# The order of VectorE's work at the second layer's first seven-product pair: one weight sum and two weight splits moved ahead of and between four output blocks

## The chip, the cores and the metric

The kernel runs on one core of one Trainium2 chip. The metric is the device time of one execution in microseconds (us); the figure for the kernel before is the median of three executions. Beside these times stands one profiled execution, of which every instruction's start and length is recorded.

## The reference, cut to what matters

The computation is one block of a network with two stages, each with a layer norm ahead of it and a modulation drawn from a small vector `c`. The first stage is a gated long convolution over the 2048 tokens. The second, in which the change lies, mixes tokens:

```python
def _B_ref(x, w1, b1, w2, b2):
    h = _layernorm(x, axis=-1)                 # (1, 2048 tokens, 640 channels)
    u = jnp.einsum("bsd,sf->bdf", h, w1) + b1  # first layer, F = 1728
    u = _gelu(u)
    y = jnp.einsum("bdf,fs->bds", u, w2) + b2  # second layer, back to 2048 tokens
    return transpose(y, 0, 2, 1)
...
h = _layernorm(x, axis=-1) * (1 + cb) + sb
x = x + gb * _B_ref(h, B_w1, B_b1, B_w2, B_b2)
```

All inputs and outputs are float32. In the kernel's second layer the output for 128 tokens and 640 channels is a product of a slice of `w2` (the stationary operand) with `u` (the moving operand), summed over 14 blocks of 128 values of F; then `b2` is added, the sum is multiplied by `gb`, and `x` is added.

## The kernel before

**Precision.** TensorE multiplies in a reduced float32 format. Each operand is therefore kept as two parts: a high part, written by ScalarE as a copy into that format, and a rest, written by VectorE as the operand less the high part. A product of two operands is three matmuls: high with high, high with rest, rest with high (`product`, L1046). Making the two parts of a weight tile is a `split` (L1034 on ScalarE, then a subtraction on VectorE). All of VectorE's two-operand work goes through one helper, so it carries line L57 whatever it computes.

**The second layer in two parts.** The 16 blocks of 128 output tokens are done in two ways. The first four (`for s in range(NW)`, matmuls on L1123) are plain products, each into a PSUM bank pair of its own, `acc[0]` to `acc[3]`. The other twelve are done two at a time, in six pairs, and each pair by seven products in place of eight (a Strassen-like scheme): the weights of a pair are cut into four blocks, A11, A12, A21 and A22, sums of them (S1 to S4) are made on VectorE, and seven products named in `ORDER` are run, 42 in all. They are numbered here as in the code, from 0: product 0 is A11, 1 is A12, 2 is S1, 3 is S2, 4 is S3, 5 is S4, 6 is A22, and product 7 begins the next pair. The change's "sixth sum" is that of product 5, its "fifth and sixth splits" those of products 4 and 5. One product is 7 blocks of F times 3 matmuls, 21 matmuls of 128x320.

**What one product needs.** `sums(n)` makes the weight sum of product n where it has one: one subtraction or addition for S1 and S4, two for S2 (which make S3's too), none for the others. `split(n)` fills one of three weight slots, slot n modulo 3, so it can start once product n - 3 is done. `product(n)` runs the matmuls into a PSUM bank. There are four banks in turn (the ring of L811); products 0 and 1 share one, 2 and 3 another. The two that hold `acc[2]` and `acc[3]` come next in turn, so product 4 writes where `acc[2]` lay and product 5 where `acc[3]` lay.

**Outputs.** `outcome(n)` combines product n's result with those before. Four of the seven products of a pair end in `finish`: add the bias, (add a partial result,) multiply by `gb`, add `x`, and issue the store on SyncE's queue. This is three VectorE instructions where a partial result is added and two where not. `acc[2]` and `acc[3]` are still to be finished when the 42 products start: that is four calls of `finish`, two instructions each, on the tiles `o2, o4, o3, o1` in turn. These are "VectorE's four blocks". The first instruction of each (L1053) is the one that reads PSUM.

**Order.** Nothing reorders the instructions: the schedule is manual, and each engine works through its instructions in the order in which the program was written, waiting on semaphores. In the loop over n, the sum of product n + 3 and the split of product n + 2 are written ahead of product n, and outcome(n) behind it. In the first pair, outcomes 0 and 2 are written behind products 1 and 3. The four finishes of `acc[2]` and `acc[3]` are written at n = 1, behind outcome 1. GpSimd makes the last set of moving sums (`t_ops(6, pool)`) as the loop begins.

Of the kernel before, what the change touches and what calls it, by code (L numbers as in the profile page):

```python
# [47 lines left out]
def mixer_kernel(ctx: ExitStack, tc: tile.TileContext, q, k, v, shift_k, ssm_k, ssm_D, w1, b1, w2, b2, c,  # L48
# [11 lines left out]
    def mem(tag, n, name=None):  # L60

        return sb.tile([128, n], F32, name=name or tag, tag=tag, bufs=1)
# [4 lines left out]
    def psum(slot=None):  # L67

        uid[0] += 1
        slot = ring[uid[0] % len(ring)] if slot is None else slot  # L70
        return psp.tile([128, 1024], F32, name=f"pst_{uid[0]}", tag=f"pst{slot}", bufs=1)
# [324 lines left out]
    def load_w(n, t=X):  # L396
        if n >= len(order):
            return
        i = order[n]
        if i < NF:  # L400
            t = j16(t)
            for b in range(2):
                sync.dma_start(t[64 * b:64 * b + 64],
                               dram(w1, 16 * b * F + fo(i), [[32 * F, 64], [F, 16], [1, 128]]))
            raw[i] = (t, [slice(0, 8), slice(8, 16)])
        else:
            t = f14(t)
            load_w2(t, i - NF, 0, 14)
            raw[i] = (t, [slice(0, 7), slice(7, 14)])
# [14 lines left out]
    def split_w(n, t2=None, eng=dve):  # L424
        if n >= len(order):
            return
        i = order[n]
        if t2 is None:
            t2 = T_wb[n % 2]
        view = j16 if i < NF else f14  # L430
        hi, lo = view(t2[:, 0:2048]), view(t2[:, 2048:4096])
        t, parts = raw.pop(i)
        for f in parts:
            act.activation(hi[:, f].bitcast(F32R), t[:, f], AF.Copy)
        for f in parts:
            TT(eng, lo[:, f].bitcast(F32R), t[:, f], hi[:, f], ALU.subtract)
        blk[i] = hi, lo
# [486 lines left out]
    def t_ops(i, eng=dve):  # L924

        def full(t, n, h):
            u = U[i + 7 * n]
            TT(eng, t, u[h], u[2 + h], ALU.add)

        def half(n, t):  # L930
            act.activation(TU[i][n][0].bitcast(F32R), t, AF.Copy)

        def rest(n, t):
            TT(eng, TU[i][n][1].bitcast(F32R), t, TU[i][n][0], ALU.subtract)

        a, b, c_ = RB
        full(a, 0, 0)
        full(b, 0, 1)
        TT(eng, a, b, a, ALU.subtract)
        half(0, a)  # L940
        full(c_, 1, 1)
        TT(eng, b, c_, b, ALU.subtract)
        half(2, b)
        TT(eng, c_, c_, a, ALU.subtract)
        half(1, c_)
        rest(0, a)
        full(a, 1, 0)
        TT(eng, a, a, c_, ALU.subtract)
        half(3, a)
        rest(2, b)  # L950
        rest(1, c_)
        rest(3, a)
# [42 lines left out]
    def load_pair(p, n0=0, n1=4):  # L995

        if p < NP:
            for n in range(n0, n1):
                w_ = ("A11", "A21", "A22", "A12")[n]
                A[p, w_] = place[(4 * p + n) % 8]  # L1000
                load_w2(A[p, w_], NW + 2 * p + int(w_[1] == "2"), 7 * int(w_[2] == "2"), 7)
# [4 lines left out]
    def x_pair(p):  # L1006
        if p < NP:
            for n in range(4):
                x_load(NW + 2 * p + n // 2, n % 2, xq[4 * (p % 2) + n])

    def sums(n):

        p, w_ = n // 7, ORDER[n % 7]
        if p >= NP:
            return
        a = lambda k: A[p, k]
        if w_ == "S1":
            A[p, w_] = S1
            TT(dve, S1, a("A21"), a("A22"), ALU.add)
        elif w_ == "S2":  # L1020
            TT(dve, a("A21"), a("A11"), a("A21"), ALU.subtract)
            TT(dve, a("A11"), S1, a("A11"), ALU.subtract)
            A[p, "S3"], A[p, "S2"] = a("A21"), a("A11")
        elif w_ == "S4":
            TT(dve, a("A12"), a("A12"), a("S2"), ALU.subtract)
            A[p, "S4"] = a("A12")

    def split(n):

        p, w_ = n // 7, ORDER[n % 7]  # L1030
        if p >= NP:
            return
        W[n] = slots[n % 3]
        act.activation(W[n][0].bitcast(F32R), A[p, w_], AF.Copy)  # L1034
        TT(dve, W[n][1].bitcast(F32R), A[p, w_], W[n][0], ALU.subtract)

    def product(n):
        w_ = ORDER[n % 7]
        if n > 4 or n % 2 == 0:
            bank["t"] = psum()  # L1040
        bank[n] = bank["t"][:, 0:320] if n > 3 or n % 2 == 0 else bank["t"][:, 512:832]
        wh, wl = W.pop(n)
        for i in range(7):
            rh, rl = moving[w_](i)
            for k, (w, r) in enumerate(((wh, rh), (wh, rl), (wl, rh))):
                pe.matmul(bank[n], w[:, i].bitcast(F32R), r.bitcast(F32R), start=i == 0 and k == 0,  # L1046
                          stop=i == 6 and k == 2)

    def finish(s, h, t, o, x, u=None):

        g = GB[:, 320 * h:320 * h + 320]
        if u is None:
            dve.scalar_tensor_tensor(o, t, B2C[:, s:s + 1], g, op0=ALU.add, op1=ALU.mult)  # L1053
        else:
            dve.scalar_tensor_tensor(o, t, B2C[:, s:s + 1], u, op0=ALU.add, op1=ALU.add)
            TT(dve, o, o, g, ALU.mult)
        TT(dve, o, o, x, ALU.add)
        sync.dma_start(out[128 * s:128 * s + 128, 320 * h:320 * h + 320], o)

    def outcome(n):  # L1060

        p, w_ = n // 7, ORDER[n % 7]
        t, s, x = bank.pop(n), NW + 2 * p, xq[4 * (p % 2):4 * (p % 2) + 4]
        if w_ == "A11":
            act.activation(p1, t, AF.Copy)
        elif w_ == "S1":
            act.activation(p5, t, AF.Copy)
        elif w_ == "A12":
            finish(s, 0, t, o1, x[0], p1)
        elif w_ == "S2":  # L1070
            TT(dve, u2, t, p1, ALU.add)
        elif w_ == "S3":
            TT(dve, u3, t, u2, ALU.add)
            TT(dve, u2, u2, p5, ALU.add)
            finish(s + 1, 1, u3, o4, x[3], p5)
            if p == NP - 1:
                TT(dve, u3, u3, GB[:, 0:320], ALU.mult)
                TT(dve, u3, u3, x[2], ALU.add)
        elif w_ == "S4":
            finish(s, 1, t, o2, x[1], u2)  # L1080
        elif p == NP - 1:
            finish(s + 1, 0, t, o3, u3)
        else:
            finish(s + 1, 0, t, o3, x[2], u3)
# [8 lines left out]
    def early(s):  # L1093

        for h in range(2):
            o, x, b2_ = RB[h], xe[2 * s + h], B2C[:, s:s + 1]
            dve.scalar_tensor_tensor(o, acc[s][:, h, 0:320], b2_, GB[:, 320 * h:320 * h + 320], op0=ALU.add, op1=ALU.mult)
            TT(dve, x, o, x, ALU.add)
            sync.dma_start(out[128 * s:128 * s + 128, 320 * h:320 * h + 320], x)

    for s in range(NW):
        i = NF + s
        acc.append(psum().rearrange("p (h m) -> p h m", h=2))
        split_w(i)
        load_w(i + 1)
        if s < 3:
            t_ops(3 + s)
        if s > 1:
            early(s - 2)
        if s == 3:  # L1110
            load_pair(1, 0, 3)
            m_w.append(mem("w1", 4096, "m_w0"))
            slots += [(q7(m_w[0], 1792 * i), q7(m_w[0], 1792 * i + 896)) for i in range(2)]
            split(0)
            split(1)
            sums(2)
            sums(3)
        wh, wl = blk[i]
        for f_ in range(NF):
            u = U[f_]  # L1120
            for k, (w, r) in enumerate(((wh, 0), (wh, 2), (wl, 0))):
                for h in range(2):
                    pe.matmul(acc[s][:, h, 0:320], w[:, f_].bitcast(F32R), u[r + h].bitcast(F32R),  # L1123
                              start=f_ == 0 and k == 0, stop=f_ == NF - 1 and k == 2)
# [9 lines left out]
    t_ops(6, pool)  # L1134
    load_pair(1, 3, 4)
    for n in range(7 * NP):
        if n:
            sums(n + 3)
        split(n + 2)
        product(n)  # L1140
        if n == 1 or n == 3:
            outcome(n - 1)
        if n != 0 and n != 2:
            outcome(n)
        if n == 1:
            for k in range(4):
                finish(2 + k // 2, k % 2, acc[2 + k // 2][:, k % 2, 0:320], (o2, o4, o3, o1)[k], xq[4 + k])
        if n == 2:
            x_pair(1)
        if n % 7 == 6:  # L1150
            load_pair(n // 7 + 2)
            x_pair(n // 7 + 2)
# [34 lines left out]
```

## Time and profile before

| | us |
|---|---|
| median of three executions | 681.57 |
| lowest and highest of them | 678.05 and 681.95 |
| the profiled execution | 683.93 |
| span of the profiled execution, first to last instruction | 682.1 |
| TensorE busy with matmuls (PE) | 629.4 |
| VectorE busy (DVE) | 498.3 |
| ScalarE busy (ACT) | 300.2 |
| GpSimd busy (POOL) | 133.9 |

PE is TensorE's matmuls, PEld its weight loads, DVE is VectorE, ACT ScalarE, POOL GpSimd, SPq SyncE's DMA queue. A row of the timeline has the start in us from the span's start, the length, engine, line, operation, tiles out<-in, shape and count (rows of one kind that follow each other are merged, so the start of the next row of that engine tells how long they held it), and in brackets how long the engine had been idle and what it waited for. A row of the table by windows has the stretch, its length, the busy time and instruction count of each engine, then the clock granted to TensorE as a share of full speed, the share of DMA time and GB/s. In this kernel `m_w` are the weight slots, `pst` PSUM banks, `m_x` the output, partial-result and x tiles, and `m_v`, `x` and `m_p` hold raw weight blocks and their sums.

### The profile page before, as it was taken

The page shows a single profiled execution, that of the slowest core. Times are in us where ns is not written, and L with a number is a line of the kernel's source. Part 1 is how long each engine was busy: PE and PEld are TensorE (multiplying, and loading weights), DVE is VectorE, ACT ScalarE, POOL GpSimd, SP SyncE. Part 2 cuts the span into 40 slices and gives each one's busy share as a digit, 9 for nine tenths or more (in the row PEclk, how much of TensorE's full clock was granted, in tenths as well). Part 3 has the DMA queues.
Part 4 walks back from the last instruction along what each step waited for, and adds up shares of the span by engine and source line. Part 5 has one row for each costly group of instructions (what it writes and reads, how often), then busy time and mean ns, then how long its engine had stood idle before and what let it go on. Part 6 is the DMA issues. An engine that isn't in the chain of part 4 may idle for free.

```text
span 682.1 us, 20757 instructions
## 1 busy us (share of the span) xinstructions
PE 629.4 (92%) x9119; PEld 598.4 (88%) x9119; DVE 498.3 (73%) x869; ACT 300.2 (44%) x483; POOL 133.9 (20%) x157
## 2 busy tenths in 40 slices
PE   6878778999999898798899999999999989999997
PEld 2877568899989897688899889999999989999997
DVE  7789589989898279798866622321689779888995
ACT  1654655646657265457654222322344133333331
POOL 6762067226134142000000000000000520000000
PEclk9998989999999799888899999999999999999999
DMA  9999797375426153440308333335441634355601
GB/s 188 219 260 274 246 179 157 91 138 121 66 65 215 35 134 104 91 97 1 62 1 154 62 63 63 62 64 115 120 136 55 197 114 124 102 167 166 184 32 38
DMA packets 166538, 81.23 MB, mean 119 GB/s; under 512 B 90830, under 2 KB 156912, under 8 KB 166448
## 3 DMA queue, kind: packets, MB, share of 16 engines
q1 hardware_dynamic: 159276, 78.32, 47.5%
q10 hardware_dynamic: 6916, 1.31, 1.1%
q8 instruction: 71, 1.16, 0.7%
q0 software_dynamic: 256, 0.28, 0.2%
q14 instruction: 19, 0.16, 0.1%
HBM read 69.40 MB, written 10.49 MB: 117 GB/s over the span
## 4 chain that ended last, share of the span: by engine, by line
PE 68%; DVE 14%; ACT 6%; DMA 5%; issue 3%; SPq 2%; POOL 1%; ACTq 0%; POOLq 0%; DVEq 0%
PE pst L445 20%; PE pst L1046 17%; PE pst L1123 7%; PE pst L223 7%; PE pst L242 6%; PE pst L271 5%; PE pst L291 3%; DVE p L57 3%; ACT z L280 2%; DMA in<-in_w_mod_dram 1%; PE pst L919 1%; DVE tap L57 1%; DMA y<-in_A_ssm_k_dram 1%; DVE sm L548 1%; DVE kt L57 1%
## 5 line engine op out<-in xcount | busy, mean ns | idle before, releaser
L242 PE MATMUL pst<-z,w 128*64 128x64 f32 x2560 | 78.4, 223 | 13.1 <-DVE p L57 6.7
L242 PEld LDWEIGHTS pst<-z,w 128*64 128x64 f32 x2560 | 76.4, 138 | 15.6 <-issue 9.1
L229 ACT ACTIVATE z<-pst 128x1024 f32<-128x1024 f32 (+2 forms) x45 | 43.1, 977 | 46.3 <-PE pst L223 46.2
L57 POOL TENSOR_TENSOR y<-p 128x256 f32<-128x256 f32 x72 | 51.3, 741 | 42.4 <-DVE p L57 42.1
L57 DVE TENSOR_TENSOR p<-pst,kt 128x512 f32<-128x512 f32 x80 | 50.7, 680 | 7.9 <-ACT kt L246 7.9
L1046 PE MATMUL pst<-r_z,m_w 128*128 128x320 f32 x222 | 42.0, 312 | 2.2 <-DVE m_w L57 2.2
L882 ACT ACTIVATE pst<-pst,sm 128x640 f32<-128x640 f32 x13 | 10.0, 767 | 75.9 <-PE pst L445 75.9
L271 PEld LDWEIGHTS pst<-v,y 32*128 32x128 f32 x1280 | 38.2, 187 | 5.4 <-issue 4.8
L271 PE MATMUL pst<-v,y 32*128 32x64 f32 x1280 | 40.1, 272 | 2.5 <-issue 2.3
L246 ACT ACTIVATE kt<-pst 128x512 f32<-128x512 f32 x40 | 24.0, 599 | 34.6 <-PE pst L242 18.7
L1034 ACT ACTIVATE m_w<-m_v 128x896 fp32r<-128x896 f32 x24 | 22.7, 951 | 36.9 <-PE pst L1046 16.8
L223 PE MATMUL pst<-v,x 128*64 128x128 f32 x512 | 34.6, 291 | 4.5 <-issue 4.0
L223 PE MATMUL pst<-v,p 128*64 128x128 f32 x640 | 36.7, 274 | 0.8 <-ACT p L168 0.8
L1046 PEld LDWEIGHTS pst<-r_z,m_w 128*128 128x128 f32 x222 | 35.2, 190 | 2.4 <-DVE m_w L57 2.4
L57 POOL TENSOR_TENSOR m_p<-u_i,r_z 128x320 f32<-128x320 f32 x1 | 0.9, 875 | 183.4 <-issue 183.4
L223 PEld LDWEIGHTS pst<-v,p 128*64 128x64 f32 x640 | 34.8, 137 | 2.1 <-ACT p L168 1.7
L57 DVE TENSOR_TENSOR tap<-tap,kt 128x512 f32<-128x512 f32 x51 | 35.5, 696 | 1.3
L223 PEld LDWEIGHTS pst<-v,x 128*64 128x64 f32 x512 | 31.1, 147 | 5.8 <-issue 5.2
L291 PEld LDWEIGHTS pst<-z,v 64*64 64x64 f32 x1280 | 23.9, 156 | 9.1 <-issue 3.8
L280 ACT ACTIVATE z<-pst 128x512 f32<-128x512 f32 x38 | 20.9, 647 | 23.3 <-PE pst L271 23.3
L291 PE MATMUL pst<-z,v 64*64 64x64 f32 x1280 | 25.3, 241 | 6.3 <-issue 2.4
L57 DVE TENSOR_TENSOR kt<-in,tap 128x512 f32<-128x512 f32 x42 | 28.8, 685 | 1.2
(308 smaller groups left out, 1507.4 us busy)
## 6 DMA issues: line engine op xcount, KB each, us to landing
x<-in_B_w_dram SPq DMA_DIRECT2D x20, 512.0 KB
m_x<-xs SPq DMA_DIRECT2D x28, 160.0 KB
out_dram<-m_x SPq DMA_DIRECT2D x28, 160.0 KB
aux<-in_A_ssm_k_dram SPq DMA_DIRECT2D x8, 512.0 KB
m_v<-in_B_w_dram SPq DMA_DIRECT2D x9, 448.0 KB
in<-in_w_mod_dram SPq DMA_DIRECT2D x4, 960.0 KB
x<-in_B_w_dram SPq DMA_DIRECT2D x7, 448.0 KB
in<-in_A_v_dram SPq DMA_DIRECT2D x22, 128.0 KB
```

Source lines behind the costliest of these rows:

```text
L57: TT = lambda eng, o, a, b, op: eng.tensor_tensor(o, a, b, op=op)
L223: pe.matmul(ps[64 * ri:64 * ri + 64, o:o + 255:2], lhs, F1[:, 128 * ri:128 * ri + 128], start=True, stop=True)
L229: act.activation(Z[:, side, t, :, k0:k1], ps.rearrange("p (a k e) -> p a k e", a=4, e=2)[:, :, k0:k1], AF.Copy)
L242: pe.matmul(ps[64 * h:64 * h + 64, o:o + 64], W2[k1 // 32][:, 2 * (k1 % 32) + ri], rhs, start=True, stop=True)
L246: act.activation(kt.rearrange("p (m i) -> p m i", i=32), pv[:, :, 1], AF.Copy)
L271: pe.matmul(pp[qd // 2][:, o:o + 64], Y[p, ri, i:i + 2].rearrange("p i k -> p (i k)"), V2[p, 64 * ri:64 * ri + 64], start=ri == 0, stop=ri ...
L280: act.activation(o, i, AF.Copy)
L291: pe.matmul(ps[64 * b:64 * b + 64, 512 * e + 64 * jj:512 * e + 64 * jj + 64], V1[p, ri, n2], T2[p, :, 32 * ri + n2], start=ri == 0, stop=r ...
L445: pe.matmul(ps[0:m, h, 0:320], w_.bitcast(F32R), r_[:, 320 * h:320 * h + 320].bitcast(F32R), start=first and i == 0, stop=last and i == 2)
L1034: act.activation(W[n][0].bitcast(F32R), A[p, w_], AF.Copy)
L1046: pe.matmul(bank[n], w[:, i].bitcast(F32R), r.bitcast(F32R), start=i == 0 and k == 0, stop=i == 6 and k == 2)
L1123: pe.matmul(acc[s][:, h, 0:320], w[:, f_].bitcast(F32R), u[r + h].bitcast(F32R), start=f_ == 0 and k == 0, stop=f_ == NF - 1 and k == 2)
```

## The change

At the last of the four plain blocks (s = 3), the sum of product 5 is made directly behind the sums of products 2 and 3. In the loop the sums are then written from n = 3 on (those that this leaves out at n = 1 and n = 2 are an empty one and the one that was moved). The split of product 4 moves from ahead of product 2 to behind product 1 and outcome 0, ahead of outcome 1. The split of product 5 moves from ahead of product 3 to behind product 2. The four finishes, all behind outcome 1 before, are written two and two: `acc[2]`'s at n = 1 behind outcome 1, `acc[3]`'s at n = 2 behind the split of product 5. No instruction is added or taken away, and no tile changes its place.

```diff
             split(0)
             split(1)
-            sums(2)
-            sums(3)
+            for n in (2, 3, 5):
+                sums(n)
...
     for n in range(7 * NP):
-        if n:
+        if n > 2:
             sums(n + 3)
-        split(n + 2)
+        if n not in (2, 3):
+            split(n + 2)
         product(n)
         if n == 1 or n == 3:
             outcome(n - 1)
+        if n == 1:
+            split(4)
         if n != 0 and n != 2:
             outcome(n)
-        if n == 1:
-            for k in range(4):
+        if n == 2:
+            split(5)
+        if n in (1, 2):
+            for k in (2 * n - 2, 2 * n - 1):
                 finish(2 + k // 2, k % 2, acc[2 + k // 2][:, k % 2, 0:320], (o2, o4, o3, o1)[k], xq[4 + k])
         if n == 2:
             x_pair(1)
```

VectorE's instructions where the kernel turns from the plain blocks to the products, before: the last two rows of the weight sums (`m_v` from `m_v` and `m_p`), then the rests of products 2 and 3 (`m_w1`, `m_w0`, each 128x896), then the first instruction of outcome 1.

```order
L57 TENSOR_TENSOR m_v_6142<-m_v_6142 128x896
L57 TENSOR_TENSOR m_v_6142<-m_p_5080,m_v_6142 128x896
L57 TENSOR_TENSOR m_w1_6636<-m_p_5080,m_w1_6636 128x896
L57 TENSOR_TENSOR m_w0_6544<-m_v_6142,m_w0_6544 128x896
L1055 SCALAR_TENSOR_TENSOR m_x_6637<-pst_138_6666,sm_81,m_x_6637 128x320
```

The same place on VectorE after the change.

```order
L57 TENSOR_TENSOR m_v_6142<-m_v_6142 128x896
L57 TENSOR_TENSOR m_v_6142<-m_p_5080,m_v_6142 128x896
L57 TENSOR_TENSOR m_v_6142<-m_v_6142 128x896
L57 TENSOR_TENSOR m_w1_6637<-m_p_5080,m_w1_6637 128x896
L57 TENSOR_TENSOR m_w0_6544<-m_v_6142,m_w0_6544 128x896 x2
L1055 SCALAR_TENSOR_TENSOR m_x_6638<-pst_138_6667,sm_81,m_x_6638 128x320
```

Product 5's sum now follows the other sums, and product 4's rest (the second of the two `m_w0` rows) stands ahead of outcome 1.

VectorE's four blocks before: `pst_136` is `acc[2]`, `pst_137` is `acc[3]`, and behind them stand product 5's sum, the rests of products 4 (`m_w0`) and 5 (`m_w1`), and outcome 3, which reads `pst_139`.

```order
L1053 SCALAR_TENSOR_TENSOR m_x_6637<-pst_136_6422,sm_81,rows_79 128x320
L57 TENSOR_TENSOR m_x_6637<-m_x_6637 128x320
L1053 SCALAR_TENSOR_TENSOR m_x_6637<-pst_136_6422,sm_81,rows_79 128x320
L57 TENSOR_TENSOR m_x_6637<-m_x_6637 128x320
L1053 SCALAR_TENSOR_TENSOR m_x_6637<-pst_137_6533,sm_81,rows_79 128x320
L57 TENSOR_TENSOR m_x_6637<-m_x_6637 128x320
L1053 SCALAR_TENSOR_TENSOR m_x_6637<-pst_137_6533,sm_81,rows_79 128x320
L57 TENSOR_TENSOR m_x_6637<-m_x_6637 128x320
L57 TENSOR_TENSOR m_v_6142<-m_v_6142 128x896
L57 TENSOR_TENSOR m_w0_6544<-m_v_6142,m_w0_6544 128x896
L57 TENSOR_TENSOR m_w1_6636<-m_v_6142,m_w1_6636 128x896
L57 TENSOR_TENSOR m_x_6637<-pst_139_6731,m_x_6637 128x320
```

The four blocks after the change.

```order
L1053 SCALAR_TENSOR_TENSOR m_x_6638<-pst_136_6422,sm_81,rows_79 128x320
L57 TENSOR_TENSOR m_x_6638<-m_x_6638 128x320
L1053 SCALAR_TENSOR_TENSOR m_x_6638<-pst_136_6422,sm_81,rows_79 128x320
L57 TENSOR_TENSOR m_x_6638<-m_x_6638 128x320
L57 TENSOR_TENSOR m_w1_6637<-m_v_6142,m_w1_6637 128x896
L1053 SCALAR_TENSOR_TENSOR m_x_6638<-pst_137_6533,sm_81,rows_79 128x320
L57 TENSOR_TENSOR m_x_6638<-m_x_6638 128x320
L1053 SCALAR_TENSOR_TENSOR m_x_6638<-pst_137_6533,sm_81,rows_79 128x320
L57 TENSOR_TENSOR m_x_6638<-m_x_6638 128x320
L57 TENSOR_TENSOR m_x_6638<-pst_139_6725,m_x_6638 128x320
```

Product 5's rest now stands between the two blocks of `acc[2]` and the two of `acc[3]`, and outcome 3 follows them directly. On TensorE, ScalarE, GpSimd and SyncE's queue the instructions stand in the same order as before.

## The prediction

> **What bounds the kernel now.** I read the page's chain of work first: its shares by engine, then by line.
>
> ```profile
> PE 68%; DVE 14%; ACT 6%; DMA 5%; issue 3%; SPq 2%; POOL 1%; ACTq 0%; POOLq 0%; DVEq 0%
> PE pst L445 20%; PE pst L1046 17%; PE pst L1123 7%; PE pst L223 7%; PE pst L242 6%; PE pst L271 5%; PE pst L291 3%; DVE p L57 3%; ACT z L280 2%; DMA in<-in_w_mod_dram 1%; PE pst L919 1%; DVE tap L57 1%; DMA y<-in_A_ssm_k_dram 1%; DVE sm L548 1%; DVE kt L57 1%
> ```
>
> The end is set by TensorE, and the products that the change concerns (L1046) are 17% of the chain. The change can shorten them only where TensorE waits. So I cut the second layer into windows, and then read who TensorE waited for in it.
>
> ```profile
> 545.00:560.00 15.00, 12.84 (x87) 12.57 (x86) 10.78 (x16) 5.55 (x10) 5.73 (x6) 0.99 0.32 106
> 560.00:580.00 20.00, 20.00 (x129) 20.00 (x128) 17.47 (x26) 6.34 (x9) 0.00 (x0) 0.92 0.44 126
> 580.00:620.00 40.00, 40.00 (x275) 40.00 (x274) 34.24 (x49) 13.97 (x17) 0.00 (x0) 1.00 0.46 135
> PE pst L1046 <- DVE m_w L57: 2.2, 1, 2.2
> ```
>
> TensorE (first figure behind the length) is busy throughout except 2.16 us before 560, and in all its 42 products it waits once, 2.2 us, for a weight rest of VectorE. The granted clock is 0.92 in the window behind the wait and 1.00 later. TensorE's timeline places it.
>
> ```profile
> 553.66 1.04 PE L1046 MATMUL pst<-r_z,m_w 128*128 128x320 f32 x6
> 556.74 0.45 PE L1046 MATMUL pst<-r_z,m_w 128*128 128x320 f32 x2
> 559.36 0.43 PE L1046 MATMUL pst<-r_z,m_w 128*128 128x320 f32 x1 [2.17 <-DVE m_w L57]
> 563.80 1.49 PE L1046 MATMUL pst<-u_i,m_w 128*128 128x320 f32 x9
> 566.88 0.60 PE L1046 MATMUL pst<-r_z,m_w 128*128 128x320 f32 x3
> ```
>
> Product 3 runs from 553.66 to 556.74 and product 5 from 563.80 to 566.88: a product is 3.08 us. Product 4 between them, of the same 21 matmuls, takes 563.80 - 556.74 = 7.06 us, 3.98 too many. Two of its matmuls run (high parts alone), then 2.17 us of gap, and the other 19 need 563.80 - 559.36 = 4.44 us where 19/21 of 3.08 is 2.79. So 1.65 us are lost behind the gap, and 0.16 in the two matmuls ahead of it. The windows tell what the 1.65 are:
>
> ```profile
> 557.20:559.30 2.10, 0.00 (x0) 0.00 (x0) 2.10 (x3) 0.88 (x2) 0.00 (x0) 1.00 0.58 180
> 559.30:563.00 3.70, 3.64 (x14) 3.64 (x15) 2.50 (x4) 1.24 (x3) 0.00 (x0) 0.54 0.50 164
> 563.00:564.00 1.00, 1.00 (x8) 1.00 (x8) 0.00 (x0) 0.14 (x1) 0.00 (x0) 0.98 0.00 0
> ```
>
> The clock fell to about half when TensorE came back and stood there some 3.5 us. What VectorE and ScalarE did meanwhile:
>
> ```profile
> 540.01 1.65 DVE L57 TENSOR_TENSOR m_v<-m_p,m_v 128x896 f32<-128x896 f32 x1
> 548.91 1.24 DVE L57 TENSOR_TENSOR m_w<-m_p,m_w 128x896 fp32r<-128x896 f32 x1 [7.26 <-ACT m_w L1034]
> 550.08 1.76 DVE L57 TENSOR_TENSOR m_w<-m_v,m_w 128x896 fp32r<-128x896 f32 x1
> 551.76 0.54 DVE L1055 SCALAR_TENSOR_TENSOR m_x<-pst,sm,m_x 128x320 f32<-128x320 f32 x1
> ...
> 553.27 0.55 DVE L1053 SCALAR_TENSOR_TENSOR m_x<-pst,sm,rows 128x320 f32<-128x320 f32 x1
> ...
> 554.26 0.54 DVE L1053 SCALAR_TENSOR_TENSOR m_x<-pst,sm,rows 128x320 f32<-128x320 f32 x1
> ...
> 556.23 0.54 DVE L1053 SCALAR_TENSOR_TENSOR m_x<-pst,sm,rows 128x320 f32<-128x320 f32 x1
> ...
> 557.22 1.08 DVE L57 TENSOR_TENSOR m_v<-m_v 128x896 f32<-128x896 f32 x1
> 558.22 2.27 DVE L57 TENSOR_TENSOR m_w<-m_v,m_w 128x896 fp32r<-128x896 f32 x2
> 560.41 0.48 DVE L57 TENSOR_TENSOR m_x<-pst,m_x 128x320 f32<-128x320 f32 x1
> 551.12 0.94 ACT L1034 ACTIVATE m_w<-m_v 128x896 fp32r<-128x896 f32 x1
> 558.42 0.95 ACT L1034 ACTIVATE m_w<-m_v 128x896 fp32r<-128x896 f32 x1 [6.36 <-DVE m_v L57]
> ```
>
> ScalarE has product 4's high part ready at 551.12 + 0.94 = 552.06. VectorE's rest for it starts only at 558.22, behind outcome 1 (551.76), the four blocks (553.27 to 557.22) and product 5's sum (557.22). It ends at about 559.30, and TensorE goes on at 559.36.
>
> **The change part by part.** Only VectorE's order changes, so I follow VectorE's row of instructions with the spacings of these rows: outcome 1 holds it 553.27 - 551.76 = 1.51 us, a block 554.26 - 553.27 = 0.99, a sum or a rest 558.22 - 557.22 = 1.00 (and its result is there after 1.08).
>
> *Product 5's sum* goes behind the instruction of 540.01, into the 7.26 us in which VectorE idled. It takes 1.08 us by the row of 557.22, or at worst 1.77 by its neighbour of 550.08, which ran beside GpSimd. Either fits; it costs nothing, and would only if that idle time shrank under 1.8 us. It leaves 1.00 us less behind the blocks, and product 5's high part no longer waits for it (the 6.36 us of ScalarE).
>
> *Product 4's rest* now follows product 3's, as soon as its high part is there: 552.1 to 553.1. The end of GpSimd's work speaks for 1.08 us here and not 1.76; both are kept for the range:
>
> ```profile
> 547.50 3.39 POOL L57 TENSOR_TENSOR m_w<-m_p,m_w 128x320 fp32r<-128x320 f32 x3
> ```
>
> GpSimd is done at 550.89. The rest is ready by 553.2, product 4 is due at 556.74: the wait goes, with 3.5 us to spare. Queued behind the moved rest are outcome 1 and the blocks, later by 553.1 - 551.76 = 1.3 us.
>
> *What is late next.* Product 4 writes into `acc[2]`'s bank, product 5 into `acc[3]`'s, so they wait for the first instruction of the second and of the fourth block. Outcome 1 runs 553.1 to 554.6, block one to 555.6, block two's first instruction to 555.6 + 0.54 = 556.15: 0.6 us ahead of product 4. Block two ends at 556.6. *Product 5's rest* stands there, 556.6 to 557.6; its high part can start when product 2 has left its slot at 553.66, so it is long done. Block three ends at 558.6, block four's first instruction at 559.1. Product 5 is due at 556.74 + 3.08 = 559.82: 0.7 us to spare. All four blocks are done at 559.6, the rest of product 6 (behind 0.4 us of outcome 3) near 561.0, product 6 is due at 562.90.
>
> Further on VectorE has no rest, and these rows tell how far it is behind:
>
> ```profile
> 564.00 0.49 DVE L57 TENSOR_TENSOR m_x<-pst,m_x 128x320 f32<-128x320 f32 x1 [2.11 <-PE pst L1046]
> ...
> 566.45 1.08 DVE L57 TENSOR_TENSOR m_w<-m_v,m_w 128x896 fp32r<-128x896 f32 x1
> ...
> 574.61 1.08 DVE L57 TENSOR_TENSOR m_w<-m_p,m_w 128x896 fp32r<-128x896 f32 x1
> 576.12 1.04 PE L1046 MATMUL pst<-r_z,m_w 128*128 128x320 f32 x6
> ```
>
> Outcome 4 takes 566.45 - 564.00 = 2.45 us, and from product 7's rest (566.45) to product 9's (574.61) VectorE works 8.16 us on end. With the change outcome 4 starts at 561.0, since its product ends near 559.9; product 7's rest starts at 563.45, product 9's at 571.6 and ends at 572.7. TensorE, without the gap, reaches product 9 at 556.74 + 5 x 3.08 = 572.14 and needs the rest in its third matmul, 2 x 3.08/21 = 0.29 later, at 572.43. So it waits 0.27 us there, where before the rest was done at 575.69, 0.7 us ahead of need. This is the new wait. At worst the rest of 552.1 takes 1.76: then it is 0.95. At best none. Behind it VectorE catches up: it is busy 34.24 of 40 us in the steady window.
>
> SyncE's stores and the x loads of the next pair keep their order. The last two stores and these loads are issued 559.6 - 557.2 = 2.4 us later, and the loads are first used by outcome 8, behind 572.7.
>
> **The sum.** Gap, slow clock and the two slowed matmuls -3.98, new wait +0.27: -3.7 us. The profiled execution, 683.93 with 1.83 around its span of 682.1, would take 680.2. The median of 681.57 lies 2.4 under that execution; taken off the median the sum gives 677.9.
>
> **The clock, weighed.** Does the fall belong to this gap? Other gaps of the profile, each with the window behind it:
>
> ```profile
> 41.50 3.70 PE L242 MATMUL pst<-z,w 128*64 128x64 f32 x119 [2.03 <-DVE p L57]
> 42.00:44.00 2.00, 2.00 (x76) 2.00 (x74) 2.00 (x4) 1.39 (x3) 1.65 (x3) 1.00 1.07 256
> 95.92 0.39 PE L291 MATMUL pst<-z,v 64*64 64x64 f32 x10 [2.38 <-issue]
> 96.00:98.00 2.00, 2.00 (x42) 1.93 (x43) 1.90 (x3) 0.00 (x0) 1.92 (x2) 1.00 0.86 188
> 226.20 3.57 PE L223 MATMUL pst<-v,x 128*64 128x128 f32 x30 [1.93 <-issue]
> 226.00:228.00 2.00, 1.80 (x18) 1.80 (x19) 0.00 (x0) 0.00 (x0) 0.00 (x0) 0.50 0.00 0
> ```
>
> Behind gaps of 2.03 and 2.38 us the clock stayed at 1.00, behind one of 1.93 it was 0.50. A gap of about 2 us thus sometimes halves it; it is no matter of length alone. In the profiled execution the 1.65 us go with the gap. In a timed execution in which the clock does not fall here, there is nothing to win but the gap.
>
> [...]
>
> **The rivals.**
>
> *The slow clock is not won* (0.2). Either the 1.65 us have another cause than the gap, or the executions that make the median have no fall here. The rows of 41.50 and 95.92 speak for it, that of 226.20 and the fall right at 559.30 against. Then -2.17 - 0.16 + 0.27 = -2.06: 679.5.
>
> *A new wait takes the place* (0.12). VectorE comes later to product 9's rest than I add up, by 1.25 us or more; TensorE then has a gap of 1.5 us there, and it may bring the half clock too. The price is 1.5 + 1.65 = 3.15, the whole -3.98 + 3.15 = -0.8: 680.7. For it speaks that VectorE runs from 564.00 without a break; against it that only one of its instructions ahead can fall beside GpSimd.
>
> *Slower* (0.03). The fourth block writes the tile that outcome 1 has filled, so it waits for that store to land, and product 5 waits for the block's bank. Before, the store was issued behind outcome 1 and the block still started at 556.23 without a wait, at most 556.23 - 553.27 = 2.96 us after outcome 1. Now it has 558.6 - 554.6 = 4.0. Only a store of over 7 us would hold product 5 more than 2.3 us, which with the half clock (1.65) takes back the 3.98. At 8 us it gives 681.57 - 3.98 + 3.3 + 1.65 = 682.5.
>
> That the change does not do what it says is not to be seen: the order has the two rests where it puts them.
>
> **How the numbers follow.** The forecast, gap and slow clock gone with a wait of 0 to 0.95 us at product 9 (677.6 to 678.5), has 0.62. With the rivals that is 0.97; 0.03 is left for a median that falls outside. The three executions of before lie 3.9 us apart, which is as much as the whole gain, and a median can fall on either side of that. I take 675.2 to 681.2: above, the second rival and 0.5; below, the forecast less 2.7, three quarters of the 3.5 us by which the lowest execution of before lies under its median. One per cent is 6.8 us, about what can be told from no change: faster by more would need almost twice the whole loss at product 4, 0.04; slower by more, 688.4, has no mechanism here that reaches it but chance, 0.02; within 1%, 0.94.
>
> **What would show it.** In the profile after: no wait of TensorE at product 4; product 4 of 3.08 us; clock 1.00 from 545 to 570; VectorE's product 4 rest ahead of outcome 1, near 552.1; product 5's L1053 instruction of block four ending 0.7 us ahead of product 5; a wait of some 0.3 us at product 9's third matmul. It would be wrong if product 4 or 5 waited for a block's bank, if product 9 waited over 1 us, or if the clock fell in this stretch without a gap.

## The result and the profile after

The changed kernel takes 678.33 us (median of 20 executions), the kernel before 681.7 us (median of 20). The ratio is 0.9951, 95% interval 0.9932 to 0.9971: about 3.3 us less, between 2.0 and 4.6. The forecast was 677.9 us, by a sum of -3.7 us.

The profiled execution took 676.37 us with a span of 674.6 us. That is 7.5 us under the span before, more than the change did: product 2 started at 550.58 before and starts at 546.62 now, so 3.96 us were gone before the first moved instruction had any effect on TensorE. I therefore measure the change from the start of product 2 to the start of product 10, which is eight products, 8 x 3.08 = 24.64 us without a loss. Before it was 579.20 - 550.58 = 28.62 us. Now it is 571.66 - 546.62 = 25.04 us: **-3.58 us**. The two rows of before, then those of after:

```profile
550.58 1.04 PE L1046 MATMUL pst<-r_z,m_w 128*128 128x320 f32 x6
579.20 1.04 PE L1046 MATMUL pst<-r_z,m_w 128*128 128x320 f32 x6
546.62 1.04 PE L1046 MATMUL pst<-r_z,m_w 128*128 128x320 f32 x6
571.66 1.04 PE L1046 MATMUL pst<-r_z,m_w 128*128 128x320 f32 x6
```

The chain of work of the changed kernel, by line:

```profile
PE pst L445 20%; PE pst L1046 16%; PE pst L1123 7%; PE pst L223 7%; PE pst L271 6%; PE pst L242 5%; DVE p L57 3%; PE pst L291 2%; POOL t L57 2%; DMA in<-in_A_k_dram 1%; ACT z L280 1%; PE pst L919 1%; PE tap L351 1%; DMA y<-in_A_ssm_k_dram 1%; DVE tap L57 1%
```

The products (L1046) went from 17% to 16%. The windows of the second layer show why:

```profile
545.00:560.00 15.00, 15.00 (x105) 15.00 (x104) 14.45 (x23) 6.19 (x8) 1.94 (x2) 1.00 0.41 129
560.00:580.00 20.00, 19.87 (x135) 19.60 (x135) 17.67 (x25) 6.48 (x8) 0.00 (x0) 1.00 0.56 160
```

TensorE is busy all through the first window, where it idled 2.16 us, and the granted clock is 1.00 in both, where the second had 0.92. In the second 0.13 us of idle time is new. TensorE's timeline of the changed kernel:

```profile
549.70 1.04 PE L1046 MATMUL pst<-r_z,m_w 128*128 128x320 f32 x6
...
552.78 0.60 PE L1046 MATMUL pst<-r_z,m_w 128*128 128x320 f32 x3
...
555.86 1.48 PE L1046 MATMUL pst<-u_i,m_w 128*128 128x320 f32 x9
...
568.18 1.44 PE L1046 MATMUL pst<-r_z,m_w 128*128 128x320 f32 x6
```

Product 4 starts at 552.78 and product 5 at 555.86, 3.08 us apart. Product 9 starts at 568.18 and product 10 at 571.66, 3.48 apart: 0.40 us are lost there, in its first six matmuls (1.44 us, where other rows of six have 1.04). VectorE's timeline of the changed kernel:

```profile
537.74 1.09 DVE L57 TENSOR_TENSOR m_v<-m_v 128x896 f32<-128x896 f32 x1
544.96 1.25 DVE L57 TENSOR_TENSOR m_w<-m_p,m_w 128x896 fp32r<-128x896 f32 x1 [6.12 <-ACT m_w L1034]
546.12 1.76 DVE L57 TENSOR_TENSOR m_w<-m_v,m_w 128x896 fp32r<-128x896 f32 x1
548.13 1.09 DVE L57 TENSOR_TENSOR m_w<-m_v,m_w 128x896 fp32r<-128x896 f32 x1 [0.24 <-ACT m_w L1034]
549.14 0.55 DVE L1055 SCALAR_TENSOR_TENSOR m_x<-pst,sm,m_x 128x320 f32<-128x320 f32 x1
...
551.65 0.54 DVE L1053 SCALAR_TENSOR_TENSOR m_x<-pst,sm,rows 128x320 f32<-128x320 f32 x1
...
552.64 1.08 DVE L57 TENSOR_TENSOR m_w<-m_v,m_w 128x896 fp32r<-128x896 f32 x1
...
554.63 0.55 DVE L1053 SCALAR_TENSOR_TENSOR m_x<-pst,sm,rows 128x320 f32<-128x320 f32 x1
...
567.63 1.08 DVE L57 TENSOR_TENSOR m_w<-m_p,m_w 128x896 fp32r<-128x896 f32 x1
```

Product 5's sum (537.74) lies in VectorE's idle time, which shrank from 7.26 to 6.12 us. Product 4's rest follows product 3's at 548.13, and outcome 1 comes behind it. The two bank releases end at 551.65 + 0.54 = 552.19 and 554.63 + 0.55 = 555.18, that is 0.59 and 0.68 us ahead of products 4 and 5. Product 9's rest ends at 568.71, 0.24 us behind the moment when the third matmul is due (568.18 + 0.29).

### The profile page after: what moved, and what is told of

Its sections match the earlier page's. It is cut to its first block, busy times and chain, and to the rows that moved or that the text cites. A ratio compares the mean times of both kernels' runs of the same rounds, so it can differ in the third digit from the quotient of the medians.

```text
span 674.6 us, 20758 instructions
## 1 busy us (share of the span) xinstructions
PE 626.2 (93%) x9119; PEld 594.7 (88%) x9119; DVE 499.5 (74%) x869; ACT 300.6 (45%) x483; POOL 134.1 (20%) x157
## 4 chain that ended last, share of the span: by engine, by line
PE 66%; DVE 16%; ACT 5%; DMA 4%; issue 3%; SPq 3%; POOL 2%; ACTq 0%; DVEq 0%; POOLq 0%
PE pst L445 20%; PE pst L1046 16%; PE pst L1123 7%; PE pst L223 7%; PE pst L271 6%; PE pst L242 5%; DVE p L57 3%; PE pst L291 2%; POOL t L57 2%; DMA in<-in_A_k_dram 1%; ACT z L280 1%; PE pst L919 1%; PE tap L351 1%; DMA y<-in_A_ssm_k_dram 1%; DVE tap L57 1%
## 5 line engine op out<-in xcount | busy, mean ns | idle before, releaser
L242 PE MATMUL pst<-z,w 128*64 128x64 f32 x2560 | 80.1, 225 | 11.0 <-DVE p L57 7.0
L242 PEld LDWEIGHTS pst<-z,w 128*64 128x64 f32 x2560 | 78.0, 140 | 13.6 <-issue 6.9
L1046 PE MATMUL pst<-r_z,m_w 128*128 128x320 f32 x222 | 41.6, 309 | 0.1
L1046 PEld LDWEIGHTS pst<-r_z,m_w 128*128 128x128 f32 x222 | 34.8, 188 | 0.4 <-DVE m_w L57 0.4
L291 PEld LDWEIGHTS pst<-z,v 64*64 64x64 f32 x1280 | 22.0, 143 | 9.4 <-issue 3.8
L57 DVE TENSOR_TENSOR m_w<-m_v,m_w 128x896 fp32r<-128x896 f32 x24 | 27.9, 1166 | 2.5 <-ACT m_w L1034 2.1
```

What stands on the lines that cost most here:

```text
L57: TT = lambda eng, o, a, b, op: eng.tensor_tensor(o, a, b, op=op)
L242: pe.matmul(ps[64 * h:64 * h + 64, o:o + 64], W2[k1 // 32][:, 2 * (k1 % 32) + ri], rhs, start=True, stop=True)
L291: pe.matmul(ps[64 * b:64 * b + 64, 512 * e + 64 * jj:512 * e + 64 * jj + 64], V1[p, ri, n2], T2[p, :, 32 * ri + n2], start=ri == 0, stop=r ...
```

## The experiments

In all of them the measure is the stretch from product 2 to product 10. It was the same to 0.03 us wherever a kernel was profiled more than once at full clock. The difference between kernels in the time of a whole execution is 0.7% at most, which 12 executions separate badly.

**The early sum alone.**

```diff
-            sums(2)
-            sums(3)
+            for n in (2, 3, 5):
+                sums(n)
...
-        if n:
+        if n > 2:
             sums(n + 3)
```

> The kernel before with one edit: product 5's sum made behind those of products 2 and 3. Theory (TensorE waits for product 4's rest, which stands behind the blocks in VectorE's row): the rest starts one VectorE instruction (1.00 us) earlier, so the gap inside product 4 goes from 2.17 to about 1.17 us, and product 5, whose high part no longer waits for the sum, has no wait; product 9 has none either, since TensorE is still later than VectorE there. Rival (the slow clock has another cause than the gap): the half clock of some 3.5 us behind product 4's start is there as before. If it is the gap's, it is there seldom or never at 1.17 us. Against the kernel before: -1.0 us with the half clock, -2.65 us without.

> The kernel before with product 5's sum made early, once more: the gap is 1.17 us, half of that before. Theory (the chance of a fall grows with the gap): full clock behind it again, product 4 takes 4.5 us. If the clock falls at this gap too, product 4 takes about 6.1 us, and what the early sum alone wins is 1.0 us and not 2.6.

TensorE's timeline of the first of the two runs, and the windows of its gap and of what follows:

```profile
553.10 0.45 PE L1046 MATMUL pst<-r_z,m_w 128*128 128x320 f32 x2
554.72 0.42 PE L1046 MATMUL pst<-r_z,m_w 128*128 128x320 f32 x1 [1.17 <-DVE m_w L57]
...
557.61 1.48 PE L1046 MATMUL pst<-u_i,m_w 128*128 128x320 f32 x9
553.50:554.70 1.20, 0.05 (x1) 0.00 (x0) 1.20 (x3) 1.07 (x2) 0.00 (x0) 1.00 0.50 186
554.70:559.00 4.30, 4.28 (x29) 4.29 (x30) 3.52 (x6) 0.95 (x1) 0.00 (x0) 1.00 0.58 179
```

The gap is 1.17 us, as expected to the hundredth, the clock stays at 1.00, and product 4 takes 557.61 - 553.10 = 4.51 us. The second run had the same gap and 4.51 us again. The stretch is 26.07 us in both: -2.55 us. One VectorE instruction of 1.00 us, moved into idle time, thus wins 71% of the change, 1.00 by the shorter gap and 1.55 by the clock that does not fall. Over 12 executions its ratio to before is 0.9933 (0.9905 to 0.996), not to be told from that of the whole change.

**Product 4's split alone.**

```diff
-        split(n + 2)
+        if n != 2:
+            split(n + 2)
         product(n)
         if n == 1 or n == 3:
             outcome(n - 1)
+        if n == 1:
+            split(4)
```

> The kernel before with one edit: product 4's split moved ahead of outcome 1. Theory: product 4 has no wait, but the place that is late moves to product 5: VectorE ends the four blocks about 6.5 us after it starts product 4's rest, then makes product 5's sum (1.1), ScalarE its high part (0.95), VectorE its rest (1.1); TensorE waits about 0.9 us ahead of product 5 and 0.8 us more in its third matmul, and 0 to 0.65 us at product 9. Against the kernel before: -1.6 us if the clock stays, -0.6 us if it falls. Rival (product 4's split alone carries the gain): product 5 has no wait, and the time is that of the changed kernel, -3.5 us.

TensorE's timeline:

```profile
564.10 0.56 PE L1046 MATMUL pst<-u_i,m_w 128*128 128x320 f32 x2 [0.80 <-ACT m_w L1034]
565.23 1.29 PE L1046 MATMUL pst<-u_i,m_w 128*128 128x320 f32 x7 [0.56 <-DVE m_w L57]
...
577.36 0.46 PE L1046 MATMUL pst<-r_z,m_w 128*128 128x320 f32 x2
578.24 0.86 PE L1046 MATMUL pst<-r_z,m_w 128*128 128x320 f32 x4 [0.43 <-DVE m_w L57]
```

Product 4 no longer waits, but product 5 waits twice, 0.80 us for its high part and 0.56 for its rest, and product 9 waits 0.43. The stretch is 581.14 - 553.90 = 27.24 us: -1.38. The wait moved as expected, and a little less came back than the 1.6 us; the ratio, 0.9981 (0.9948 to 1.0014), is not clear of no change. The rival, that this split alone carries the gain, falls.

**All four blocks ahead of product 5's split.**

```diff
-        if n in (1, 2):
-            for k in (2 * n - 2, 2 * n - 1):
+        if n == 1:
+            for k in range(4):
                 finish(...)
```

> The changed kernel with one part undone: all four blocks stand ahead of product 5's split. Theory (each step has its spare): product 5's rest then ends about 0.2 us ahead of product 5's start, 0.45 us ahead of its third matmul, block four's first instruction 1.7 us ahead; no wait at products 4 and 5, and everything from outcome 3 on stands as in the changed kernel, with the same 0.4 us at product 9. Difference from the changed kernel 0.0 us. Rival (the split between the blocks is needed): a wait at product 5 of some tenths of a us.

The first row of product 2, and that of product 10:

```profile
548.01 1.04 PE L1046 MATMUL pst<-r_z,m_w 128*128 128x320 f32 x6
...
573.05 1.04 PE L1046 MATMUL pst<-r_z,m_w 128*128 128x320 f32 x6
```

The stretch is 573.05 - 548.01 = 25.04 us, that of the changed kernel, with no wait at products 4 and 5. Parting the blocks two and two is worth nothing here: product 5's rest is in time behind all four. The ratio to before is 0.9955 (0.9927 to 0.9983).

**`acc[3]`'s blocks still later.** Only the order is changed: the two finishes of `acc[3]` and the x loads of the next pair, which overwrite what these finishes read, stand behind product 4 and ahead of outcome 4.

```diff
-        if n != 0 and n != 2:
+        if n in (0, 2, 4):
+            pass
+        else:
             outcome(n)
...
-        if n in (1, 2):
-            for k in (2 * n - 2, 2 * n - 1):
+        if n in (1, 4):
+            for k in ((0, 1) if n == 1 else (2, 3)):
                 finish(...)
+        if n == 4:
+            outcome(n)
-        if n == 2:
+        if n == 4:
             x_pair(1)
```

> The changed kernel with acc[3]'s two blocks moved behind product 4, ahead of outcome 4 (and the loads of the next pair's x with them). Theory (product 5 cannot start before the first instruction of block four has read its bank): that instruction now stands behind product 6's rest and ends about 1.0 us after product 5 is due, so TensorE waits about 1.0 us between products 4 and 5; product 9 then has no loss, since TensorE is later and VectorE as before. Against the changed kernel +0.6 us if the clock stays at full. Rival (the bank does not bind, only the rests do): product 5 starts on time, and product 9 loses the 0.4 us as in the changed kernel.

The rows of VectorE, of ScalarE and of TensorE there:

```profile
558.85 0.55 DVE L1053 SCALAR_TENSOR_TENSOR m_x<-pst,sm,rows 128x320 f32<-128x320 f32 x1
552.32 0.95 ACT L1034 ACTIVATE m_w<-m_v 128x896 fp32r<-128x896 f32 x1 [1.66 <-PE pst L1046]
559.54 1.56 PE L1046 MATMUL pst<-u_i,m_w 128*128 128x320 f32 x9 [0.96 <-ACT m_w L1034]
562.70 0.60 PE L1046 MATMUL pst<-r_z,m_w 128*128 128x320 f32 x3
```

TensorE waits 0.96 us ahead of product 5. The row puts it down to ScalarE's high part, but that was done at 553.27; what ends just ahead of 559.54 is the fourth block's first instruction, at 559.40. The bank binds, then. In the changed kernel that instruction ends 0.68 us ahead of product 5; since TensorE went on 0.14 us behind it here, some 0.5 us of this could be used up (an estimate). The stretch is 575.02 - 549.18 = 25.84 us, 0.80 above the changed kernel's, where +0.6 was expected: the instruction ends 0.97 us after product 5 is due, as worked out, but the stop costs 1.20 us; product 9 takes 575.02 - 571.94 = 3.08 us, as expected. With product 5 late, product 9's loss went away, so the two waits are alternatives.

**The split ahead of the sum.**

```diff
-        if n > 2:
-            sums(n + 3)
         if n not in (2, 3):
             split(n + 2)
+        if n > 2:
+            sums(n + 3)
         product(n)
```

> The changed kernel with one edit: in the loop the split of product n + 2 stands ahead of the sum of product n + 3. Theory (product 9's loss of 0.4 us is VectorE making S2's two sums, 2.1 us, ahead of product 9's rest): the rest is ready 2 us earlier and product 9 takes 3.08 us instead of 3.48; the later products have no waits. Against the changed kernel -0.4 us. Rival (VectorE's sum of work over the first pair is the bound, not its order): a wait of about the same size turns up at product 10 or 11.

Product 2's first row, product 9's and product 10's:

```profile
546.14 1.04 PE L1046 MATMUL pst<-r_z,m_w 128*128 128x320 f32 x6
...
567.70 1.04 PE L1046 MATMUL pst<-r_z,m_w 128*128 128x320 f32 x6
...
570.78 1.04 PE L1046 MATMUL pst<-r_z,m_w 128*128 128x320 f32 x6
```

The stretch is 570.78 - 546.14 = 24.64 us, eight products without a loss, and TensorE waits for nothing from there to its end. So product 9's 0.40 us came from the order, S2's two sums ahead of product 9's rest, and not from VectorE's sum of work. By the stretch this version beats the changed kernel by 0.40 us. Its time, 677.94 us over 12 executions (ratio to before 0.9951, 0.9919 to 0.9983), cannot show 0.06%.

**Does the gap make the clock fall?** First the gap filled: 14 extra matmuls, whose results are not used, between the second and third matmul of product 4 in the kernel before.

```diff
             for k, (w, r) in enumerate(((wh, rh), (wh, rl), (wl, rh))):
+                if n == 4 and i == 0 and k == 2:
+                    for _ in range(14):
+                        pe.matmul(bank["t"][:, 512:832], wh[:, 0]..., rh..., start=True, stop=True)
```

> The kernel before, with 14 extra matmuls of 128x320 put between the second and the third matmul of product 4, into an unused part of its bank; they need nothing that is late and fill some 2.05 us of the 2.17 us gap. Theory (the idle gap makes the clock fall): the clock stays at full behind it, product 4 with the extra matmuls takes about 3.08 + 2.2 = 5.3 us. Rival (the slow stretch has another cause): half clock for some 3.4 us behind 559 as before, about 7 us.

> The kernel before with the 14 extra matmuls in product 4's gap once more, since the first profile of it ran at a lower clock throughout. Theory (the idle gap makes the clock fall): full clock behind product 4, which takes with its extra matmuls about 3.08 + 2.2 = 5.3 us. Rival (another cause): half clock for some 3.4 us, about 7 us.

The first of these took 714.5 us, with a mean granted clock of 0.837 over the whole execution, where the other profiles have 0.965 to 0.982. The rows are the second's:

```profile
555.55 0.45 PE L1049 MATMUL pst<-r_z,m_w 128*128 128x320 f32 x2
555.84 2.22 PE L1048 MATMUL pst<-r_z,m_w 128*128 128x320 f32 x14
...
561.06 1.48 PE L1049 MATMUL pst<-u_i,m_w 128*128 128x320 f32 x9
555.80:558.00 2.20, 2.20 (x16) 1.99 (x14) 2.20 (x3) 0.78 (x1) 0.00 (x0) 1.00 0.56 182
558.00:562.00 4.00, 3.89 (x27) 3.84 (x27) 3.30 (x6) 2.23 (x4) 0.00 (x0) 1.00 0.49 152
```

The clock stays at 1.00, and product 4 takes 561.06 - 555.55 = 5.51 us instead of 7.06, with 14 matmuls more. Then the kernel before, profiled four times more:

> The kernel before, unchanged, profiled again. [...] Rival (the fall belongs to this place): 7.1 us each time.

> The kernel before a third time, with the same expectations as for the second: 7.1 us for product 4 with the half clock, about 5.4 us without, the gap of 2.17 us in either.

> The kernel before a fourth time; three profiles had the half clock behind the gap. [...] Rival (the fall comes each time at a gap of 2.17 us): 7.1.

> The kernel before a fifth time, as the fourth: 7.1 us for product 4 with the half clock, about 5.4 without; the theory of chance wants at least one of the five without.

Of the second and the fourth profile, the gap's end and a window behind it:

```profile
561.63 0.41 PE L1046 MATMUL pst<-r_z,m_w 128*128 128x320 f32 x1 [2.19 <-DVE m_w L57]
561.40:565.20 3.80, 3.57 (x15) 3.57 (x16) 2.67 (x4) 1.41 (x3) 0.00 (x0) 0.59 0.51 170
```

```profile
554.33 0.64 PE L1046 MATMUL pst<-r_z,m_w 128*128 128x320 f32 x1 [2.17 <-DVE m_w L57]
554.40:557.80 3.40, 3.40 (x13) 3.40 (x14) 2.46 (x3) 1.10 (x2) 0.00 (x0) 0.51 0.49 153
```

All five profiles of the kernel before have the half clock behind this gap of 2.17 to 2.19 us; product 4 takes 7.04 to 7.07 us and the stretch 28.60 to 28.63 in each. With the gap filled (the second profile of the two), cut to 1.17 us (two profiles) or gone from product 4 (the changed kernel, product 4's split alone and `acc[3]`'s blocks later), the windows behind product 4 have a clock of 1.00. In the two other versions without the gap, all four blocks ahead and the split ahead of the sum, products 4 and 5 take 3.08 us each. That the fall belongs to the gap is shown; the other cause falls. The theory of chance, by which the clock falls behind this gap in some executions and not in others, wanted at least one of the five without the fall, and there is none. That does not rule chance out: the last section has a gap of 2.48 us that halved the clock in one profile and not in another.

## Why the prediction was right, point by point

- *The gap* (-2.17) and *the slow matmuls ahead of it* (-0.16): gone. Product 4 takes 3.08 us, as said.
- *The slow clock* (-1.65): gone with the gap. I gave 0.2 to its not being won, from two gaps of the profile behind which the clock had stayed. At this place it fell in five profiles of five, and the filled gap (clock 1.00) shows the idle time to be its cause. The cause was right; by the five profiles the chance was rather too large. Two readings behind it were not right. The row of 226.20 does not show a fall behind a gap of 1.93 us: the clock had fallen at 225.12 already, 1.08 us before TensorE came back. And 0.10 of the 1.65 us is not the clock's: with the early sum alone, at a clock of 1.00, the same 19 matmuls took 557.61 - 554.72 = 2.89 us, where 2.79 was worked out. It is gone all the same, since TensorE no longer stops there.
- *Product 5's sum at no cost*: it took 1.09 us of the idle time.
- *The two bank releases*: 0.6 and 0.7 us of spare were worked out, 0.59 and 0.68 measured. That the bank is what would bind next is shown by the blocks moved later, where TensorE waited 0.96 us.
- *The new wait at product 9*: 0.27 us worked out, 0.40 lost. The place and VectorE's time were right: the rest was to start at 571.6 on the clock of the profile before, which is 567.64 with the 3.96 us taken off, and it started at 567.63. The step that was too small is the restart. I counted only the time by which the rest is late, 0.24 as measured. Besides, TensorE goes on at 568.77, 0.06 us after the rest is there, and loses 0.10 more behind that. The same two pieces show at product 4: before, the rest ends at 559.30 and TensorE goes on at 559.36, and with the early sum alone the 0.10 above are lost behind it.
- *The sum*: -3.7 worked out, -3.58 in the stretch, -3.3 (-4.6 to -2.0) in the timed executions.
- *Rivals*: no wait of over 1 us came at product 9, and the fourth block did not wait for outcome 1's store.
- One reading the prediction did not make: the parts of the change are far from equal. The early sum alone wins 2.55 us, the moved split alone 1.38, and the parting of the blocks nothing.

## What to carry to other kernels

Look at a gap of the bounding engine together with the clock behind it: here 2.17 us idle cost 3.98 us, and the cheapest edit, one instruction moved into idle time, won 2.55 of it: behind the 1.17 us of gap that it left, the clock stayed at 1.00 in both profiles. When an instruction is moved ahead of a wait, follow its engine's row on to the next two or three deadlines; the spares there (0.6, 0.7 and -0.24 us) could be worked out to 0.03 us from one profile. Where a loop makes next-but-two work ahead of next-but-one work on a shared engine, the order itself can cost time though the engine has room, here 0.40 us at product 9.

## What the runs showed of the hardware

The same length of gap does not always have the same effect. The matmuls of the first layer (L445) have a gap of 2.48 us in both kernels. Here it is before, with three windows:

```profile
308.93 8.84 PE L445 MATMUL pst<-r_v,wb 128*128 128x320 f32 x48 [2.48 <-ACT r_v L775]
307.04:310.45 3.41, 1.52 (x10) 1.52 (x11) 2.39 (x7) 2.48 (x5) 0.00 (x0) 1.00 0.01 2
310.45:313.86 3.41, 3.41 (x15) 3.41 (x14) 3.34 (x8) 2.95 (x4) 0.00 (x0) 0.50 0.02 5
313.86:317.28 3.42, 3.42 (x25) 3.42 (x24) 2.45 (x11) 1.92 (x6) 0.41 (x2) 1.00 0.00 0
```

After the change, at the same place of the program:

```profile
304.97 7.33 PE L445 MATMUL pst<-r_v,wb 128*128 128x320 f32 x48 [2.48 <-ACT r_v L775]
303.21:306.62 3.41, 1.65 (x11) 1.65 (x12) 2.51 (x8) 2.53 (x4) 0.00 (x0) 1.00 0.01 2
306.62:310.03 3.41, 3.41 (x25) 3.41 (x24) 3.34 (x8) 2.95 (x5) 0.00 (x0) 1.00 0.02 5
```

One halved the clock and the other did not: the same 48 matmuls took 8.84 us and 7.33. Before, the half clock lasted from 310.45 to 313.86, that is 3.41 us, and the rows are cut to this length. At product 4 it lasted as long, from 559.62 to 563.03. The windows ahead of this and of it are:

```profile
556.21:559.62 3.41, 1.25 (x9) 0.98 (x8) 3.28 (x6) 1.20 (x3) 0.00 (x0) 1.00 0.58 192
559.62:563.03 3.41, 3.41 (x14) 3.41 (x14) 2.27 (x3) 0.92 (x2) 0.00 (x0) 0.50 0.45 145
```

Nor does the longer of two gaps always halve the clock. In the version with the split ahead of the sum, the one of 2.18 us did, and the one of 2.76 us left it at 1.00:

```profile
304.49 7.69 PE L445 MATMUL pst<-r_v,wb 128*128 128x320 f32 x40 [2.18 <-ACT r_v L775]
304.81:305.06 0.25, 0.25 (x2) 0.25 (x2) 0.25 (x1) 0.25 (x1) 0.00 (x0) 0.50 0.00 0
323.19 2.61 PE L445 MATMUL pst<-h_a,wb 128*128 128x320 f32 x16 [2.76 <-ACT h_a L775]
323.43:323.68 0.25, 0.25 (x3) 0.25 (x3) 0.25 (x1) 0.25 (x1) 0.00 (x0) 1.00 1.19 207
```

In the changed kernel the same 16 matmuls have a gap of 2.76 us too. There the clock was 0.50 from 323.69 to 327.10, and they took 4.15 us in place of 2.61. The gap at product 4, 2.17 to 2.19 us, halved the clock five times of five; the fall came 0.02 to 0.85 us after TensorE went on. The gap of 1.17 us there did not in either of its two profiles. What decides between a fall and none is left open: no run moves one gap and leaves all else as it is.

A fall does not always cost time either. The 3.96 us by which the two profiles differ ahead of the change were there before the fall of 310.45, for 308.93 - 304.97 is 3.96 too, so the fall added nothing to them. After the change the next 48 matmuls, at 313.58, wait 1.28 us for ScalarE; before, at 317.62, they came later and did not wait.
